# Layernorm in pieces between evictions, one range wrap per table pair, and half-wise hazards in the C scaling of an S5 and Mish kernel

## The chip, the cores and the metric

The kernel runs on one core of one Trainium2 chip. The metric is the device time of one execution in microseconds, and lower is better. Kernels that were sent together ran on the same chip and share their runs of the kernel before.

## The reference, cut to what matters

```python
xn = layernorm(x)                                   # x: 1 x 2048 x 1024, bf16
dt, Lam = exp(log_dt), Lambda_re + 1j * Lambda_im   # 1024 states
Lam_bar = exp(dt * Lam)
Bu = xn @ (((Lam_bar - 1) / Lam)[:, None] * B).T    # B, C complex
h[t] = Lam_bar * h[t-1] + Bu[t]                     # scan over 2048 steps
y = 2 * (h @ C.T).real + xn * Dskip
u = xn @ w1 + b1                                    # 1024 -> 3584 (the B_ half, on the same xn)
out = x + y + (u * tanh(softplus(u))) @ w2
```

## The kernel before

The sequence is handled in four blocks of 512 steps. A block has four stages on TensorE: 28 tiles of first matmuls (8 matmuls each, 224 in all), the projection by B (8 state tiles of 16 matmuls), the second matmuls (224) and the output projection by C (128). VectorE adds the bias to each tile of the first stage while it moves it out of PSUM (`hb`); this move is called the tile's eviction below. ScalarE makes Mish in four groups of seven tiles: Exp, Ln(1 + .), Tanh. The complex recurrence is turned into a real scan by rotating with tables of cosine and sine (`tab`).

The first block has extra work, which a function `side(f)` inserts after tile `f`: the skip product, the next block's layernorm, coefficients, tables, and the transposes of B and C. This is the part that the change rewrites:

```python
def side(f):
    if blk == 0:
        if f == 0:
            for q in range(NQ): ln_skip(0, q)
        if f == 1:
            ln_stats(1, 0); ln_stats(1, 1); ln_apply(1, 0)      # ... the other quarters likewise
            coefficients()
        if f == GF - 1:                      # GF = 7: after Mish group 0 was queued
            for j in range(5): table(j)
            for j in range(5, NJ): phases(j)
        if f == 3 * GF - 1:                  # after Mish group 2
            for j in range(5, NJ): table(j)
        # ... transposes of B (f < 16) and C (f >= 16) on the sync queue

def first_tile(f):
    # 8 matmuls into PSUM bank f % 8 ...
    if f % GF == 0 and f >= 2 * GF:
        mish_mul(f // GF - 2)                # VectorE; waits for ScalarE's Mish of that group
    vop(lambda e: e.tensor_scalar(hb[:, hs, :], ps[:, bank, :], b1(f), None, op0=ALU.add), ...)
    if f % GF == GF - 1:
        mish(f // GF)                        # ScalarE
```

The tables need an angle wrapped into half a turn to either side, which GpSimd does in three operations, for sine and cosine separately:

```python
def phases(j):
    for s in range(2):
        turn = 0.25 if s == 0 else 0.0
        pop(... px = iot * thp[j] + turn)                     # tensor_scalar, mult and add
        pop(... py = (px + ROUND_MAGIC) - ROUND_MAGIC)
        pop(... dst = px - py)
```

The C scaling makes, per state tile and half, two copies on ScalarE and two products on VectorE. Its three buffers rotate, and its hazards (which operation must wait for which, because they touch the same data) are tracked for the whole state tile `b_CT[j]`:

```python
def scale_C(j):
    for h in range(2):
        ta, b_ta = ct[n_ct[0] % 3]; tb, b_tb = ct[(n_ct[0] + 1) % 3]; n_ct[0] += 2
        aop(ta = cim * nci2[j], reads=[b_CT[j], ...], writes=[b_ta])
        aop(tb = cre * nci2[j], reads=[b_CT[j], ...], writes=[b_tb])
        vop(cre = cre * cr2[j] + ta, reads=[b_CT[j], b_ta], writes=[b_CT[j]])
        vop(cim = cim * ncr2[j] + tb, reads=[b_CT[j], b_tb], writes=[b_CT[j]])
```

## Time and profile before

The time before is 678.91 us, the median of three runs (678.77 to 678.99). The span of the profiled run is 676.4 us.

| engine | busy, us | share of the span |
|---|---|---|
| TensorE (PE) | 621.5 | 92% |
| VectorE (DVE) | 478.6 | 71% |
| ScalarE (ACT) | 247.7 | 37% |
| GpSimd (POOL) | 74.9 | 11% |

TensorE is the bound, and what can be gained lies in the time in which it waits. The page's chain that ended last, as shares of the span by engine, says how much of the end was set by others:

```profile
PE 73%; DVE 17%; ACT 7%; issue 1%; DMA 1%; POOL 0%; DVEq 0%; ACTq 0%; POOLq 0%
```

A quarter of the chain is on VectorE and ScalarE. Apart from the last 1.2 us of the run, all of that is in the first block and its start, as the prediction shows with TensorE's waits and timeline.

### The profile page before, as it was taken

To read this page: it belongs to the slowest core of one execution; us is meant where nothing else is said; L and a number is where in the kernel's file an instruction comes from. 1 tells how busy PE (TensorE), PEld (TensorE's weight loads), DVE (VectorE), ACT (ScalarE), POOL (GpSimd) and SP (SyncE) were. 2 spreads that over 40 slices of the span, in tenths; PEclk is the share of its full clock that TensorE was granted. 3 is DMA by queue.
4 is the path that set the end of the run, shared out by engine and by line. 5 is a ranking of instruction groups with operands and counts; after the bars stand their busy time and mean duration, and the time that the engine had idled before them with its cause. 6 is when DMAs were issued, how large, how long until landed. Compare 5 with 4: busy or idle time off the path is not lost.

```text
span 676.4 us, 7254 instructions
## 1 busy us (share of the span) xinstructions
PE 621.5 (92%) x2849; PEld 280.4 (41%) x2849; DVE 478.6 (71%) x718; ACT 247.7 (37%) x163; POOL 74.9 (11%) x74
## 2 busy tenths in 40 slices
PE   0583979999968999999999999999999999999997
PEld 0231434444423444444444444444444444444443
DVE  4698519988887455999983455999983455999702
ACT  2103999722220499500000499500000499400000
POOL 7995360000001000000000000000000000000000
PEclk9995999999997999999999999999999999999999
DMA  9594996077302653019623654018521543014001
GB/s 286 102 211 101 214 245 133 0 194 191 114 0 83 189 155 134 1 60 213 163 63 96 179 156 128 1 65 215 157 63 63 156 155 125 1 65 153 1 0 63
DMA packets 124018, 79.40 MB, mean 117 GB/s; under 512 B 48898, under 2 KB 106256, under 8 KB 123984
## 3 DMA queue, kind: packets, MB, share of 16 engines
q1 hardware_dynamic: 120224, 70.79, 39.5%
q10 hardware_dynamic: 2592, 4.72, 1.9%
q0 software_dynamic: 1168, 3.42, 1.6%
q8 instruction: 23, 0.38, 0.2%
q14 instruction: 11, 0.09, 0.0%
HBM read 63.19 MB, written 4.19 MB: 100 GB/s over the span
## 4 chain that ended last, share of the span: by engine, by line
PE 73%; DVE 17%; ACT 7%; issue 1%; DMA 1%; POOL 0%; DVEq 0%; ACTq 0%; POOLq 0%
PE ps L602 35%; PE ps L526 22%; PE ps L546 16%; DVE hT L566 3%; DVE CT L487 2%; DVE CT L484 2%; DVE stats L337 2%; DVE mt L571 2%; ACT tab L428 1%; DVE xn L354 1%; ACT act L508 1%; ACT act L506 1%; ACT act L507 1%; ACT ct L480 1%; DMA st<-in_B_b_dram 1%
## 5 line engine op out<-in xcount | busy, mean ns | idle before, releaser
L526 PE MATMUL ps<-xnT,ring 128*128 128x512 bf16 x896 | 199.2, 386 | 15.4 <-issue 14.4
L602 PE MATMUL ps<-ring,act 128*128 128x512 bf16 x896 | 194.0, 379 | 0.0
L526 PEld LDWEIGHTS ps<-xnT,ring 128*128 128x128 bf16 x896 | 88.7, 99 | 125.1 <-issue 22.4
L533 DVE TENSOR_SCALAR hb<-ps,par 128x512 bf16<-128x512 f32 x112 | 81.8, 749 | 75.5 <-PE ps L526 74.7
L602 PEld LDWEIGHTS ps<-ring,act 128*128 128x128 bf16 x896 | 87.7, 98 | 105.7
L602 PE MATMUL ps<-CT,hT 128*128 128x512 bf16 x512 | 113.7, 384 | 9.1 <-DVE CT L487 9.1
L546 PE MATMUL ps<-xnT,BT 128*128 128x512 bf16 x512 | 112.7, 382 | 4.4 <-DVE hb L533 4.4
L551 DVE TENSOR_TENSOR mt<-ps,tab 128x1024 bf16<-128x1024 f32 x64 | 75.3, 1219 | 11.4 <-PE ps L546 9.9
L602 PEld LDWEIGHTS ps<-CT,hT 128*128 128x128 bf16 x512 | 50.5, 99 | 71.7 <-DVE CT L487 10.1
L546 PEld LDWEIGHTS ps<-xnT,BT 128*128 128x128 bf16 x512 | 50.4, 99 | 66.0 <-DVE hb L533 4.9
L506 ACT ACTIVATE act<-hb 128x3584 bf16<-128x3584 bf16 x16 | 50.9, 3180 | 50.1 <-DVE hb L533 50.1
L635 DVE TENSOR_TENSOR xx<-ps,xx 128x1024 bf16<-128x1024 f32 x16 | 19.5, 1224 | 56.8 <-PE ps L602 56.7
L566 DVE TENSOR_TENSOR_SCAN hT<-cs,qi,hT 128x512 bf16<-128x512 f32 x48 | 58.9, 1269 | 0.0
L506 ACT ACT_TABLE_LOAD x5 | 6.4, 1283 | 124.4 <-PE ps L526 124.3
L507 ACT ACTIVATE act<-act 128x3584 bf16<-128x3584 bf16 x16 | 51.0, 3190 | 0.2
L508 ACT ACTIVATE act<-act 128x3584 bf16<-128x3584 bf16 x16 | 51.0, 3190 | 0.2
L513 DVE TENSOR_TENSOR act<-act,hb 128x3584 bf16<-128x3584 bf16 x16 | 32.4, 2023 | 20.0 <-ACT act L508 20.0
L571 DVE TENSOR_TENSOR mt<-hT,tab 128x1024 bf16<-128x1024 bf16 x64 | 41.4, 689 | 1.1
L286 POOL DMA_DIRECT2D xx<-in_A_x_dram x12 | 6.6, 553 | 273.0 <-DVE xx L635 265.4
L342 ACT ACTIVATE rs<-rs 128x1 f32<-128x1 f32 x16 | 3.2, 203 | 91.7 <-DVE rs L340 91.7
L420 POOL TENSOR_SCALAR py<-px 128x512 f32<-128x512 f32 x16 | 31.1, 1944 | 1.4
L480 ACT ACTIVATE ct<-CT,cs 128x512 f32<-128x512 bf16 x16 | 11.4, 714 | 51.0 <-DVE CT L487 51.0
(63 smaller groups left out, 306.0 us busy)
## 6 DMA issues: line engine op xcount, KB each, us to landing
ring<-in_B_w_dram SPq DMA_DIRECT2D x112, 512.0 KB, 3.8
out_dram<-xx ACTq DMA_DIRECT2D x16, 256.0 KB, 2.0
xx<-in_A_x_dram POOLq DMA_DIRECT2D x12, 256.0 KB, 4.1
xx<-in_A_x_dram SPq DMA_DIRECT2D x2, 256.0 KB, 3.8
xx<-in_A_x_dram ACTq DMA_DIRECT2D x2, 256.0 KB, 4.1
dsk<-in_A_Dskip_dram POOLq DMA_DIRECT2D x1, 256.0 KB, 6.7
xnT<-xn SPq DMA_TRANSPOSE x12, 4.6
BT<-in_A_B_re_dram SPq DMA_TRANSPOSE x8, 4.9
```

The source lines that it names most:

```text
L420: pop(lambda e: e.tensor_scalar(py[:], px[:], ROUND_MAGIC, ROUND_MAGIC, op0=ALU.add, op1=ALU.subtract), reads=[b_px], writes=[b_py])
L506: aop(lambda e: e.activation(a, hs, AF.Exp), reads=[b_hb[g % 2]], writes=[b_act[g]])
L507: aop(lambda e: e.activation(a, a, AF.Ln, bias=1.0), reads=[b_act[g]], writes=[b_act[g]])
L508: aop(lambda e: e.activation(a, a, AF.Tanh), reads=[b_act[g]], writes=[b_act[g]])
L513: vop(lambda e: e.tensor_tensor(a, a, hs, op=ALU.mult), reads=[b_act[g], b_hb[g % 2]], writes=[b_act[g]])
L526: PE.mm(lambda e, k=k: e.matmul(ps[:, bank, :], lhsT=wt[:, k, fi * P:(fi + 1) * P], rhs=xnT[:, k, :], start=k == 0, stop=k == NK - 1), rea ...
L533: vop(lambda e: e.tensor_scalar(hb[:, hs, :], ps[:, bank, :], b1(f), None, op0=ALU.add), reads=[b_ps[bank], b_par], writes=[b_hbf[hs]])
L546: PE.mm(lambda e, j=j, ci=ci, k=k, bank=bank: e.matmul(ps[:, bank + ci, :], lhsT=BT[:, ci, j, k, :], rhs=xnT[:, k, :], start=k == 0, stop= ...
L551: vop(lambda e, s=s, u=u, j=j: e.tensor_tensor(mt[:, s, :, :], u, tab[:, s, j, :].unsqueeze(1).to_broadcast([P, 2, TB]), op=ALU.mult), rea ...
L566: vop(lambda e, ci=ci, init=init: e.tensor_tensor_scan(out=hT[:, ci, j, :], data0=cj("r", j).to_broadcast([P, TB]), data1=hT[:, ci, j, :], ...
L571: vop(lambda e, s=s: e.tensor_tensor(mt[:, s, :, :], hT[:, :, j, :], tab[:, s, j, :].unsqueeze(1).to_broadcast([P, 2, TB]), op=ALU.mult), ...
L602: PE.mm(lambda e: e.matmul(ps[:, u, :], lhsT=lhsT, rhs=rhs, start=st_, stop=last), reads=reads, writes=[b_ps[u]], first=st_, last=last)
```

## The change

The intent is to keep TensorE fed in block 0. The layernorm of block 1 and the coefficients go in small pieces between evictions; the square root of the layernorms of blocks 1 to 3 leaves ScalarE; one wrap serves both tables of a pair, with the cosine as sin(pi/2 - 2 pi |x|), which costs an Abs on ScalarE; three table pairs come before Mish 0; and the C scaling gets hazards per half and seven buffers.

```diff
-    b_CT = [Buf("CT%d" % j) for j in range(NJ)]
+    b_CT = [Buf("CT%d" % j, parts=[Buf("CT%d_%d" % (j, h)) for h in range(2)]) for j in range(NJ)]
 ...
+    def ln_stats_only(blk, q): ...      # bn_stats twice, bn_aggr
+    def ln_rsqrt(): ...                 # 1/sqrt of all four quarters by shift and three Newton steps, VectorE
+    def ln_scale(blk, q): ...           # (x - mean) * rsqrt
 ...
     def phases(j):
-        for s in range(2):
-            turn = 0.25 if s == 0 else 0.0
-            pop(... tensor_scalar(px, iot, thp[j], turn, op0=mult, op1=add))
-            pop(... tensor_scalar(py, px, ROUND_MAGIC, ROUND_MAGIC, op0=add, op1=subtract))
-            pop(... dst = px - py)
+        pop(... tensor_scalar(px, iot, thp[j], None, op0=mult))
+        pop(... tensor_scalar(py, px, ROUND_MAGIC, -ROUND_MAGIC, op0=add, op1=add))
+        pop(... xs = px - py)
     def table(j):
-        for s in range(2): aop(tab[s, j] = Sin(2 pi * ph[j, s]))
+        aop(tab[1, j] = Sin(2 pi * src))
+        aop(src = Abs(src))
+        aop(tab[0, j] = Sin(-2 pi * src + pi / 2))
 ...
     def scale_C(j):                      # buffers: 3 -> NCT = GF = 7
-                reads=[b_CT[j], ...], writes=[b_CT[j]]
+                reads=[b_CT[j].parts[h], ...], writes=[b_CT[j].parts[h]]
 ...
         def side(f):
-            # f == 0: four skips; f == 1: whole layernorm of block 1, all coefficients
-            # f == 6: tables 0 to 4; f == 20: tables 5 to 7
+            if f < NQ: ln_skip(0, f)
+            if f == 4: coefficients(0)
+            if f == 5: tables 0 to 2            # queued before Mish 0
+            if f == 7: tables 3 to 7            # queued after Mish 0
+            if 6 <= f < 9: coefficients(f - 5)
+            if f in (9, 10, 11, 12): ln_stats_only(1, f - 9)
+            if f == 13: ln_rsqrt()
+            if f in (16, 17, 18, 19): ln_scale(1, f - 16)
 ...                                       # blocks 1 and 2 use the new layernorm form too
```

More of the change, by code (lines that the diff above doesn't have):

```diff
@@ L11 @@
 TWO_PI = 6.283185
+HALF_PI = 1.5707963
 ROUND_MAGIC = 12582912.0
@@ L268, in build_kernel, with ph_slot @@
     ph = [scratch("ph_%s%d" % w, w[0], w[1], f32, TB)
-          for w in (("h", 2), ("h", 3), ("h", 6), ("h", 7), ("a", 11), ("a", 12), ("a", 13),
-                    ("h", 0), ("h", 1), ("h", 4), ("h", 5))]
-    def ph_slot(j, s):
-        return ph[(2 * j + s) % len(ph)]
+          for w in (("h", 0), ("h", 1), ("h", 2), ("h", 3), ("h", 6), ("h", 7), ("a", 11), ("a", 12))]
+    def ph_slot(j):
+        return ph[j]
     vop, aop, pop = VE.op, AC.op, PO.op
@@ L325, in build_kernel @@
                                   compare_op=ALU.is_equal, fill=0.0), reads=[b_ident], writes=[b_ident])
-    pop(lambda e: e.memset(kon[:, 1:2], 0.0), writes=[b_kon])
+    pop(lambda e: e.memset(kon[:, 0:1], HALF_PI), writes=[b_kon])
+    pop(lambda e: e.memset(kon[:, 1:2], 0.0), reads=[b_kon], writes=[b_kon])
     pop(lambda e: e.iota(iot_i[:], pattern=[[1, TB]], base=0, channel_multiplier=0), writes=[b_iot_i])
@@ L356, in ln_apply, with ln_stats_only, ln_rsqrt, ln_scale @@
             reads=[b_xx[i][q], b_mv[q], b_rs[q]], writes=[b_xn[q]])
+    rv = [sb("rv%d" % i, [P, NQ], f32 if i < 3 else i32) for i in range(4)]
+    b_rv = [Buf("rv%d" % i) for i in range(4)]
+    def ln_stats_only(blk, q):
+        i, s = blk % 2, q % 2
+        for h in range(2):
+            vop(lambda e, h=h: e.bn_stats(stats[:, s, h, :], xx[:, i, q, h * 512:(h + 1) * 512]),
+                reads=[b_xx[i][q]], writes=[b_stats[s]])
+        vop(lambda e: e.bn_aggr(mv[:, q, :], stats[:, s, :, :]), reads=[b_stats[s]], writes=[b_mv[q]])
+    def ln_rsqrt():
+        v, y, t = (rv[n][:, :] for n in range(3))
+        yi, vi, b_i = rv[1][:, :].bitcast(i32), rv[0][:, :].bitcast(i32), rv[3][:, :]
+        vop(lambda e: e.tensor_scalar(v, mv[:, :, 1], EPS, None, op0=ALU.add), reads=b_mv, writes=[b_rv[0]])
+        vop(lambda e: e.tensor_scalar(b_i, vi, 1, None, op0=ALU.logical_shift_right),
+            reads=[b_rv[0]], writes=[b_rv[3]])
+        vop(lambda e: e.tensor_scalar(yi, b_i, -1.0, float(0x5f3759df), op0=ALU.mult, op1=ALU.add),
+            reads=[b_rv[3]], writes=[b_rv[1]])
+        for _ in range(3):
+            vop(lambda e: e.tensor_tensor(t, y, y, op=ALU.mult), reads=[b_rv[1]], writes=[b_rv[2]])
+            vop(lambda e: e.tensor_tensor(t, t, v, op=ALU.mult), reads=[b_rv[0], b_rv[2]], writes=[b_rv[2]])
+            vop(lambda e: e.tensor_scalar(t, t, -0.5, 1.5, op0=ALU.mult, op1=ALU.add),
+                reads=[b_rv[2]], writes=[b_rv[2]])
+            vop(lambda e: e.tensor_tensor(y, y, t, op=ALU.mult), reads=[b_rv[1], b_rv[2]], writes=[b_rv[1]])
+    def ln_scale(blk, q):
+        i = blk % 2
+        vop(lambda e: e.tensor_scalar(xn[:, q, :], xx[:, i, q, :], mv[:, q, 0:1], rv[1][:, q:q + 1],
+                                      op0=ALU.subtract, op1=ALU.mult),
+            reads=[b_xx[i][q], b_mv[q], b_rv[1]], writes=[b_xn[q]])
     def ln_skip(blk, q):
@@ L414, in phases @@
     def phases(j):
-        for s in range(2):
-            dst, b_dst = ph_slot(j, s)
-            turn = 0.25 if s == 0 else 0.0
-            pop(lambda e, turn=turn: e.tensor_scalar(px[:], iot[:], cj("thp", j), turn, op0=ALU.mult, op1=ALU.add),
-                reads=[b_iot, b_cs["thp"]], writes=[b_px])
-            pop(lambda e: e.tensor_scalar(py[:], px[:], ROUND_MAGIC, ROUND_MAGIC, op0=ALU.add, op1=ALU.subtract),
-                reads=[b_px], writes=[b_py])
-            pop(lambda e, dst=dst: e.tensor_tensor(dst[:], px[:], py[:], op=ALU.subtract),
-                reads=[b_px, b_py], writes=[b_dst])
@@ L425, in table @@
-    def table(j):
-        for s in range(2):
-            src, b_src = ph_slot(j, s)
-            aop(lambda e, s=s, src=src: e.activation(tab[:, s, j, :], src[:], AF.Sin, scale=TWO_PI, bias=kon[:, 1:2]),
-                reads=[b_src, b_kon], writes=[b_tab[j]])
-    def coefficients():
-        smalls("ys", "thp", ROUND_MAGIC, ROUND_MAGIC, ALU.add, ALU.subtract)
+        xs, b_xs = ph_slot(j)
+        pop(lambda e: e.tensor_scalar(px[:], iot[:], cj("thp", j), None, op0=ALU.mult),
+            reads=[b_iot, b_cs["thp"]], writes=[b_px])
@@ new lines, in phases @@
+        pop(lambda e: e.tensor_scalar(py[:], px[:], ROUND_MAGIC, -ROUND_MAGIC, op0=ALU.add, op1=ALU.add),
+            reads=[b_px], writes=[b_py])
+        pop(lambda e: e.tensor_tensor(xs[:], px[:], py[:], op=ALU.subtract),
+            reads=[b_px, b_py], writes=[b_xs])
+    def table(j):
+        src, b_src = ph_slot(j)
+        aop(lambda e: e.activation(tab[:, 1, j, :], src[:], AF.Sin, scale=TWO_PI, bias=kon[:, 1:2]),
+            reads=[b_src, b_kon], writes=[b_tab[j]])
+        aop(lambda e: e.activation(src[:], src[:], AF.Abs), reads=[b_src], writes=[b_src])
+        aop(lambda e: e.activation(tab[:, 0, j, :], src[:], AF.Sin, scale=-TWO_PI, bias=kon[:, 0:1]),
+            reads=[b_src, b_kon], writes=[b_tab[j]])
@@ L433, in coefficients, with turns @@
+    def turns():
+        smalls("ys", "thp", ROUND_MAGIC, -ROUND_MAGIC, ALU.add, ALU.add)
         small("xs", "thp", "ys", ALU.subtract)
-        smalls("xc", "thp", 0.25, None, ALU.add, ALU.bypass)
-        smalls("yc", "xc", ROUND_MAGIC, ROUND_MAGIC, ALU.add, ALU.subtract)
-        small("xc", "xc", "yc", ALU.subtract)
+        smalls("xc", "xs", -1.0, None, ALU.mult, ALU.bypass)
+        small("xc", "xs", "xc", ALU.max)
         aop(lambda e: e.activation(c("s1"), c("xs"), AF.Sin, scale=TWO_PI, bias=kon[:, 1:2]),
@@ L438, in coefficients @@
             reads=[b_cs["xs"], b_kon], writes=[b_cs["s1"]])
-        aop(lambda e: e.activation(c("c1"), c("xc"), AF.Sin, scale=TWO_PI, bias=kon[:, 1:2]),
+        aop(lambda e: e.activation(c("c1"), c("xc"), AF.Sin, scale=-TWO_PI, bias=kon[:, 0:1]),
             reads=[b_cs["xc"], b_kon], writes=[b_cs["c1"]])
-        small("lr", "r", "c1", ALU.mult)
-        small("li", "r", "s1", ALU.mult)
-        smalls("nr", "lr", -1.0, None, ALU.add, ALU.bypass)
-        small("den", lre, lre, ALU.mult)
@@ L446, in coefficients @@
-        small("t1", lim, lim, ALU.mult)
-        small("den", "den", "t1", ALU.add)
-        vop(lambda e: e.reciprocal(c("inv"), c("den")), reads=[b_cs["den"]], writes=[b_cs["inv"]])
-        small("t1", "nr", lre, ALU.mult)
-        small("t2", "li", lim, ALU.mult)
-        small("t1", "t1", "t2", ALU.add)
-        small("t1", "t1", "inv", ALU.mult)
-        smalls("cr2", "t1", 2.0, None, ALU.mult, ALU.bypass)
-        smalls("ncr2", "t1", -2.0, None, ALU.mult, ALU.bypass)
-        small("t1", "li", lre, ALU.mult)
@@ L456, in coefficients @@
-        small("t2", "nr", lim, ALU.mult)
-        small("t1", "t1", "t2", ALU.subtract)
-        small("t1", "t1", "inv", ALU.mult)
-        smalls("nci2", "t1", -2.0, None, ALU.mult, ALU.bypass)
+    def coefficients(part):
+        if part == 0:
+            small("den", lre, lre, ALU.mult)
+            small("t1", lim, lim, ALU.mult)
+            small("den", "den", "t1", ALU.add)
+            vop(lambda e: e.reciprocal(c("inv"), c("den")), reads=[b_cs["den"]], writes=[b_cs["inv"]])
+        if part == 1:
+            small("lr", "r", "c1", ALU.mult)
+            small("li", "r", "s1", ALU.mult)
+            smalls("nr", "lr", -1.0, None, ALU.add, ALU.bypass)
+        if part == 2:
+            small("t1", "nr", lre, ALU.mult)
+            small("t2", "li", lim, ALU.mult)
+            small("t1", "t1", "t2", ALU.add)
+            small("t1", "t1", "inv", ALU.mult)
+            smalls("cr2", "t1", 2.0, None, ALU.mult, ALU.bypass)
+            smalls("ncr2", "t1", -2.0, None, ALU.mult, ALU.bypass)
+        if part == 3:
+            small("t1", "li", lre, ALU.mult)
+            small("t2", "nr", lim, ALU.mult)
+            small("t1", "t1", "t2", ALU.subtract)
+            small("t1", "t1", "inv", ALU.mult)
+            smalls("nci2", "t1", -2.0, None, ALU.mult, ALU.bypass)
@@ L461, in build_kernel @@
+    turns()
     for j in range(NJ):
-        if j == 5:
-            break
         phases(j)
     base_hb = nc.lookup_mloc(hb).addr
-    ct = []
-    for i in range(3):
-        ct.append((nc.alloc_sbuf_tensor_at("ct%d" % i, [P, HB], f32, offset=base_hb + 2048 * i),
-                   Buf("ct%d" % i, parts=b_hbf[2 * i:2 * i + 2])))
+    NCT = GF
+    ct = [(nc.alloc_sbuf_tensor_at("ct%d" % i, [P, HB], f32, offset=base_hb + 2048 * i),
+           Buf("ct%d" % i, parts=b_hbf[2 * i:2 * i + 2])) for i in range(NCT)]
@@ L476, in scale_C @@
             cre, cim = (CT[:, ci, j, h * HB:(h + 1) * HB] for ci in range(2))
-            ta, b_ta = ct[n_ct[0] % 3]
-            tb, b_tb = ct[(n_ct[0] + 1) % 3]
+            b_c = b_CT[j].parts[h]
+            ta, b_ta = ct[n_ct[0] % NCT]
+            tb, b_tb = ct[(n_ct[0] + 1) % NCT]
             n_ct[0] += 2
             aop(lambda e, ta=ta, cim=cim: e.activation(ta[:], cim, AF.Copy, scale=cj("nci2", j)),
-                reads=[b_CT[j], b_cs["nci2"]], writes=[b_ta])
+                reads=[b_c, b_cs["nci2"]], writes=[b_ta])
             aop(lambda e, tb=tb, cre=cre: e.activation(tb[:], cre, AF.Copy, scale=cj("nci2", j)),
-                reads=[b_CT[j], b_cs["nci2"]], writes=[b_tb])
+                reads=[b_c, b_cs["nci2"]], writes=[b_tb])
             vop(lambda e, ta=ta, cre=cre: e.scalar_tensor_tensor(
                 out=cre, in0=cre, scalar=cj("cr2", j), in1=ta[:], op0=ALU.mult, op1=ALU.add),
-                reads=[b_CT[j], b_ta, b_cs["cr2"]], writes=[b_CT[j]])
+                reads=[b_c, b_ta, b_cs["cr2"]], writes=[b_c])
             vop(lambda e, tb=tb, cim=cim: e.scalar_tensor_tensor(
                 out=cim, in0=cim, scalar=cj("ncr2", j), in1=tb[:], op0=ALU.mult, op1=ALU.add),
-                reads=[b_CT[j], b_tb, b_cs["ncr2"]], writes=[b_CT[j]])
+                reads=[b_c, b_tb, b_cs["ncr2"]], writes=[b_c])
     def transpose_B(j):
@@ L647, in side @@
         def side(f):
-            if blk == 0:
-                if f == 0:
-                    for q in range(NQ):
-                        ln_skip(0, q)
-                if f == 1:
-                    ln_stats(1, 0)
-                    ln_stats(1, 1)
-                    ln_apply(1, 0)
-                    ln_stats(1, 2)
-                    ln_apply(1, 1)
-                    ln_stats(1, 3)
-                    ln_apply(1, 2)
-                    ln_apply(1, 3)
-                    coefficients()
-                if f == GF - 1:
-                    for j in range(5):
-                        table(j)
-                    for j in range(5, NJ):
-                        phases(j)
-                if f == 3 * GF - 1:
-                    for j in range(5, NJ):
-                        table(j)
-                if f < 16 and f % 2 == 0:
-                    transpose_B(f // 2)
-                if f >= 16:
-                    transpose_C(f - 16)
+            if blk:
+                return
+            if f < NQ:
+                ln_skip(0, f)
+            if f == 4:
+                coefficients(0)
+            if f == 5:
+                for j in range(3):
+                    table(j)
+            if f == 7:
+                for j in range(3, NJ):
+                    table(j)
+            if 6 <= f < 9:
+                coefficients(f - 5)
+            if f in (9, 10, 11, 12):
+                ln_stats_only(1, f - 9)
+            if f == 13:
+                ln_rsqrt()
+            if f in (16, 17, 18, 19):
+                ln_scale(1, f - 16)
+            if f < 16 and f % 2 == 0:
+                transpose_B(f // 2)
+            if f >= 16:
+                transpose_C(f - 16)
         for f in range(NF):
@@ L683, in build_kernel @@
             for q in range(NQ):
-                ln_stats(blk + 1, q)
-                if q:
-                    ln_apply(blk + 1, q - 1)
-            ln_apply(blk + 1, NQ - 1)
+                ln_stats_only(blk + 1, q)
+            ln_rsqrt()
+            for q in range(NQ):
+                ln_scale(blk + 1, q)
         for j in range(NJ):
```

## The prediction

> **What bounds the kernel now.** I read the busy slices first, then TensorE's waits and timeline, then the clock in chosen windows, then VectorE's and ScalarE's timelines around each hole. TensorE is busy 92% of the span, and its timeline shows the last three blocks (216.5 us to the end) as one unbroken stream: 48.35 us of first matmuls, 27.6 of projection, 48.35 of second matmuls, 27.6 of output projection, 152 us a block, with no wait. So blocks 1 to 3 can't get shorter by anything in this diff. The waits of TensorE (waiter, releaser: total us, times, longest) all lie in block 0 and its start:
>
> ```profile
> PE ps L526 <- issue: 14.4, 1, 14.4
> PE ps L404 <- DVE xn L354: 13.6, 4, 7.1
> PE ps L602 <- DVE CT L487: 9.1, 2, 7.8
> PE ps L546 <- DVE hb L533: 4.4, 1, 4.4
> ```
>
> Its timeline (start, length, work, idle before it) places the holes:
>
> ```profile
> 27.47 19.99 PE L526 MATMUL ps<-xnT,ring 128*128 128x512 bf16 x80 [0.99 <-DVE xnT L411]
> 61.84 33.69 PE L526 MATMUL ps<-xnT,ring 128*128 128x512 bf16 x144 [14.38 <-issue]
> 95.36 1.89 PE L546 MATMUL ps<-xnT,BT 128*128 128x512 bf16 x8
> 101.64 27.41 PE L546 MATMUL ps<-xnT,BT 128*128 128x512 bf16 x120 [4.38 <-DVE hb L533]
> ...
> 205.69 11.01 PE L602 MATMUL ps<-CT,hT 128*128 128x512 bf16 x40 [7.80 <-DVE CT L487]
> ```
>
> The 14.4 us hole follows the tenth tile. "issue" hides its cause: eight PSUM banks plus the two evicted ones are used up, and VectorE does all of the next layernorm and the coefficients from 39.63 to 61.08 before it evicts tile 2, at 60.99, just before TensorE goes on.
>
> The 4.4 us hole: tile 21's eviction stands behind the Mish product of group 1, which waits for ScalarE. ScalarE's timeline between the two Mish groups is full:
>
> ```profile
> 64.41 3.19 ACT L506 ACTIVATE act<-hb 128x3584 bf16<-128x3584 bf16 x1 [4.68 <-DVE hb L533]
> ...
> 76.62 1.28 ACT L428 ACT_TABLE_LOAD   x1
> 77.91 2.96 ACT L428 ACTIVATE tab<-ph_h,kon 128x512 bf16<-128x512 f32 x4
> ...
> 86.47 3.19 ACT L506 ACTIVATE act<-hb 128x3584 bf16<-128x3584 bf16 x1
> ```
>
> The 9.1 us hole (1.3 and 7.8) is the scaling of C. VectorE spends 8.83 us per state tile in recurrence and scaling, of which 1.47 is a wait for ScalarE, eight times:
>
> ```profile
> 140.03 0.75 DVE L487 SCALAR_TENSOR_TENSOR CT<-CT,cs,ct 128x512 bf16<-128x512 bf16 x1
> 142.26 0.75 DVE L484 SCALAR_TENSOR_TENSOR CT<-CT,cs,ct 128x512 bf16<-128x512 bf16 x1 [1.47 <-ACT ct L482]
> 143.05 0.75 DVE L487 SCALAR_TENSOR_TENSOR CT<-CT,cs,ct 128x512 bf16<-128x512 bf16 x1
> 143.72 2.33 DVE L566 TENSOR_TENSOR_SCAN hT<-cs,hT 128x512 bf16<-128x512 f32 x2
> ```
>
> Each hole also costs clock afterwards. The windows (stretch, length, busy us and count per engine, granted clock) right after the two long holes:
>
> ```profile
> 61.80:66.00 4.20, 4.16 (x10) 1.49 (x11) 4.20 (x7) 1.59 (x1) 0.00 (x0) 0.50 0.00 0
> 205.70:210.00 4.30, 4.30 (x11) 1.54 (x12) 4.09 (x12) 0.00 (x0) 0.00 (x0) 0.50 0.01 4
> ```
>
> **What the Trainium skill says.** (1) TensorE: Matmul & The Clock Gate, section "What's actually happening": after an idle window of about 3.4 us the array runs at half clock until about 3.4 us of activity. The trace agrees: clock 0.50 and 10 or 11 matmuls in 4.2 us, where the steady rate is 48.35/224 = 0.216 us each. So 144 matmuls took 33.5 us from start to the next group's start against 31.1, and the last 40 took 10.84 against 8.63: 2.4 and 2.2 us lost. (2) ScalarE: Activation LUTs, section "Table sets: the hidden batching unit": the tables are loaded by set, and cheap functions, copy and abs among them, are in every set. Copy agrees: the scaling copies start at 129.75 straight after Tanh, without a load. Abs doesn't occur before the change, so no run shows it yet. A load takes 1.28 us here. (3) SBUF — State Buffer, section "Who interferes with whom": a VectorE instruction with two SBUF inputs contends with GpSimd reads. The trace agrees: the four skip additions L364 took 0.69, 1.64, 0.98 and 0.69 us while GpSimd was at its range wraps.
>
> **The change part by part.**
>
> *Layernorm and coefficients in pieces.* VectorE's new side work is 4 skips (one after each of tiles 0 to 3), 4 small operations after tile 4, 14 in three portions after tiles 6 to 8, statistics of one quarter (two of 0.7 us and one of 0.2, so 1.7 with gaps) after each of tiles 9 to 12, 15 chained small operations of about 0.19 after tile 13, and four normalizations of 0.6 to 0.9 after tiles 16 to 19. With 14 evictions of 0.67 (9.4), the skips as measured with GpSimd beside them (31.83 to 39.05: 7.2), 18 small at 0.18 (3.2), 4 x 1.7 (6.8) and 2.8, VectorE needs 29.4 us up to tile 13, from 31.1 to 60.5. A tile takes TensorE 8 x 0.216 = 1.73 us, so it finishes tile 13 at 27.47 + 2.56 + 14 x 1.73 = 54.2 (2.56 is the cold start: 80 matmuls lasted 19.83 in place of 17.27). VectorE is 6 us behind at worst, 3.6 tiles, against eight banks. So the 14.4 us hole and the 2.4 us of cold clock go away whole: 16.8.
>
> *Tables.* Removed on GpSimd: one wrap of three operations per table pair (48 operations become 24), off the path. Added on ScalarE: one Abs per pair. Three pairs move before Mish 0, into free time: ScalarE is free from 26.2, runs the two small sines, then 3 x 2.15 = 6.5 us, and is done near 36. Five pairs remain between Mish 0 and Mish 1. In the old trace 10 sines took 7.26 us (a dependent one 0.73, an independent one 0.61). In the new code all three operations of a pair depend on each other, Abs being in place, so a pair takes 0.61 + 2 x 0.73 + gaps = 2.15, and five take 10.8. That is 3.5 us more than before.
> Mish 0 starts with the eviction of tile 6: 31.1 + 7 x 0.67 + 7.2 + 0.7 = 43.7. From there: 12.2 (three activations of 3.19 and two loads, to the end), 1.3 load, 10.8 tables, 1.3 load, 12.2 Mish 1: 37.8, so 81.5. Product and eviction of tile 21 took 2.94 before TensorE restarted (98.70 to 101.64), so bank 5 is free at 84.5. TensorE, no longer held up, finishes tile 27 at 27.47 + 2.56 + 28 x 1.73 = 78.4 and the first half of state tile 0 at 80.1. The **new hole is 84.5 - 80.1 = 4.4 us**, as long as the old one: TensorE and ScalarE both move forward. This part gives nothing by itself, but the projection starts at 84.5 in place of 101.64, 17.1 earlier, its own warm-up unchanged.
>
> *C scaling.* Hazards per half and seven buffers in place of three let ScalarE run ahead, so the 1.47 us go: 8.83 becomes 2.37 + 1.33 + 0.67 (recurrence) + 4 x 0.74 = 7.35 per state tile. VectorE enters the recurrence at 134.88 - 17.1 = 117.8 and ends state tile 7 at 117.8 + 8 x 7.35 = 176.6. TensorE's second matmuls end at 177.22 - 17.1 = 160.1, and it first needs state tile 7 after 80 + 8 more matmuls, at 160.1 + 88 x 0.216 = 179.1. So 2.5 us are in hand and the 9.1 us hole closes, with its 2.2 us of cold clock: 11.3.
>
> *Layernorm of blocks 1 and 2.* 36 VectorE instructions in 12.2 us (298.26 to 310.48) become 31 in 4 x 1.7 + 2.8 + 4 x 0.5 = 11.6, and ScalarE loses its Sqrt and its loads. TensorE waits for none of it: 0.
>
> **Sum.** 160.1 + 128 x 0.216 = 187.7 for the end of block 0, where block 1 began at 216.53: 28.8 us. By terms: 14.4 + 2.4 + 0 + 9.1 + 2.2 = 28.1. I take 28.6: 678.9 - 28.6 = 650.3.
>
> **Rivals.**
> 1. *Abs reloads tables.* If Sin and Abs were not in one set here, each of the five pairs would cost two loads more: 12.8 us. Mish 1 would end at 94.3 and the hole be 17 us: near 663. The skill speaks against it; only copy is shown. Chance 4%.
> 2. *Scaling stays in step.* If VectorE kept 8.83 per state tile (say, by buffers that come free late), it would end at 117.8 + 70.6 = 188.4, 9.3 us after TensorE wants it, with a cold restart: near 661. Against it: four ScalarE copies cost 2.7 us per state tile, far under 7.35, and ScalarE has been idle since Mish 3.
> 3. *Transfers become the bound.* From 33.74 to 56 the sync queue issued one weight load and two transposes per 4.4 us; TensorE without holes uses one weight load per 3.45 us. If the ring had no lead, block 0 would lose 13 x 0.95 = 12 us: 662. For it: DMA is at 1.1 of its mark there and SP issues back to back. Against it: seven items are loaded ahead; the eighth is issued at 33.7 and wanted at 54, the fourteenth is issued near 60 and wanted at 75, and the C transposes end near 100, before the 117 at which they are scaled. Hidden, by my count.
> 4. *ScalarE gets through sooner.* If the skips meet fewer GpSimd reads, Mish 0 starts near 42.7, and the hole falls under 3.4 us and may keep its clock warm: 648.
>
> **Range and chances.** The two large terms rest on measured holes with margins of several microseconds; the open term is the hole before the projection, 3 to 6 us with or without a cold restart (2 us). That gives 647 to 654. Rivals 1 to 3 together have some 8% and end between 661 and 664, still over 2% faster (that line is 665.3). Faster 0.95, same 0.04, slower 0.01.
>
> **What would show it.** Right: TensorE's waits list one hole of 3 to 6 us at the projection, released by the eviction of tile 21, and no 14 us one; Sin, Abs and Sin of a pair at 0.6 to 0.73 each without a load between; VectorE at some 7.35 us per state tile without a ScalarE wait; blocks 1 to 3 unchanged at 152 us. Wrong: a weight-ring or transpose wait in block 0, loads before Abs, a wait for the C scaling in the output projection, or a hole between tiles 8 and 20.

## The result, and the profile after

The changed kernel took 649.22 us (median of 4 runs, 648.98 to 650.07), beside 678.95 us for the kernel before (four runs, one more than above). The ratio is 0.9563, with a 95% interval of 0.9547 to 0.958. The predicted value was 650.3.

The chain that ended last, of the changed kernel, is now almost all TensorE:

```profile
PE 92%; DVE 4%; ACT 2%; DMA 1%; issue 0%; POOL 0%; DVEq 0%; POOLq 0%
```

Within block 0's four stages TensorE has one wait left that is longer than 1 us (waiter, releaser: total us, times, longest). L585 is the projection and L565 the first matmuls, which were L546 and L526:

```profile
PE ps L585 <- DVE hb L572: 5.9, 1, 5.9
```

Its timeline in block 0 (start, length, work, idle before it):

```profile
25.44 50.51 PE L565 MATMUL ps<-xnT,ring 128*128 128x512 bf16 x224 [0.99 <-DVE xnT L444]
75.79 1.89 PE L585 MATMUL ps<-xnT,BT 128*128 128x512 bf16 x8
83.61 28.01 PE L585 MATMUL ps<-xnT,BT 128*128 128x512 bf16 x120 [5.93 <-DVE hb L572]
111.45 48.51 PE L641 MATMUL ps<-ring,act 128*128 128x512 bf16 x224
159.80 27.79 PE L641 MATMUL ps<-CT,hT 128*128 128x512 bf16 x128
```

The hole after the tenth tile is gone, and so is the one in the output projection. The hole before the projection is still there, and it is longer: 5.93 us in place of 4.38. Stage by stage, from the starts in the two timelines:

| stage of block 0 | before, us | after, us | gain, us |
|---|---|---|---|
| up to the first matmul | 27.47 | 25.44 | 2.03 |
| first matmuls, 224 | 67.89 | 50.35 | 17.54 |
| projection by B | 33.52 | 35.66 | -2.14 |
| second matmuls | 48.34 | 48.35 | -0.01 |
| output projection by C | 39.31 | 27.63 | 11.68 |
| block 0 | 216.53 | 187.43 | 29.10 |

Blocks 1 to 3 and the end took 676.4 - 216.53 = 459.9 us before and 647.2 - 187.43 = 459.8 after. The whole gain is in block 0.

ScalarE's timeline of the changed kernel between Mish 0 and Mish 1 shows the new pair (Sin, Abs, Sin), with one table load ahead of the five pairs:

```profile
55.58 1.28 ACT L460 ACT_TABLE_LOAD   x1
56.88 0.72 ACT L460 ACTIVATE tab<-ph_h,kon 128x512 bf16<-128x512 f32 x1
57.63 0.63 ACT L462 ACTIVATE ph_h<-ph_h 128x512 f32<-128x512 f32 x1
58.30 0.72 ACT L463 ACTIVATE tab<-ph_h,kon 128x512 bf16<-128x512 f32 x1
...
67.15 1.28 ACT L545 ACT_TABLE_LOAD   x1
68.44 3.19 ACT L545 ACTIVATE act<-hb 128x3584 bf16<-128x3584 bf16 x1
```

No load stands between Sin and Abs. The pairs fill 56.88 to 67.13: five in 10.25 us. The activation that starts at 68.44 is the first of Mish 1, and ScalarE did not stop for a moment between Mish 0 and Mish 1.

The chain in order of time reads differently at this point. It puts the wait for Mish 1 down to an eviction (start, us, what):

```profile
67.79 0.67 DVE hb L572
68.46 3.17 ACT act L545
```

That is a coincidence of times. This eviction, of tile 20, ends at 68.45, a hundredth of a microsecond after the activation had begun; Mish 1 reads tiles 7 to 13, the last of which was moved out by 57.01. What the activation came after was ScalarE's own table load, which ends at 68.43. The experiments with the tables settle this.

VectorE's timeline in the C scaling of the changed kernel has no wait left:

```profile
122.36 0.75 DVE L526 SCALAR_TENSOR_TENSOR CT<-CT,cs,ct 128x512 bf16<-128x512 bf16 x1
123.03 0.75 DVE L523 SCALAR_TENSOR_TENSOR CT<-CT,cs,ct 128x512 bf16<-128x512 bf16 x1
123.81 0.75 DVE L526 SCALAR_TENSOR_TENSOR CT<-CT,cs,ct 128x512 bf16<-128x512 bf16 x1
124.48 2.33 DVE L605 TENSOR_TENSOR_SCAN hT<-cs,hT 128x512 bf16<-128x512 f32 x2
```

From this scan to the next one, at 131.76, are 7.28 us, in place of 8.83.

One thing had not been foreseen: the first matmul starts 2.03 us sooner. The chain in order of time shows where. These are the normalizations of the first three quarters of block 0's own layernorm, before:

```profile
14.86 0.94 DVE xn L354
...
19.00 0.94 DVE xn L354
...
23.14 0.94 DVE xn L354
```

and after:

```profile
15.11 0.55 DVE xn L355
...
18.17 0.55 DVE xn L355
...
21.35 0.55 DVE xn L355
```

A quarter took 4.14 us before and takes 3.06 to 3.18 now, though its VectorE code is the same. Only what GpSimd does beside it was changed. Two small operations of VectorE in the trace of before, and the GpSimd operations of the same moments, show what they waited for:

```profile
13.38 0.66 DVE L349 SCALAR_TENSOR_TENSOR rs<-rs 128x1 f32<-128x1 f32 x1
...
14.26 0.56 DVE L353 TENSOR_TENSOR rs<-rs 128x1 f32<-128x1 f32 x1
```

```profile
12.76 1.26 POOL L422 TENSOR_TENSOR ph_h<-px,py 128x512 f32<-128x512 f32 x1
14.13 0.69 POOL L418 TENSOR_SCALAR px<-iot,cs 128x512 f32<-128x512 f32 x1
```

The first ends at 14.04 and the second at 14.82, when the GpSimd operation beside it ends (14.02 and 14.82). With no GpSimd work, in the layernorms that run during blocks 1 and 2, the same operations take 0.22 and 0.16 us, the normalization 0.55 in place of 0.94, and a whole quarter 3.05 (302.62 to 305.67).

### The profile page after: what moved, and what is told of

Read it like the earlier page. It is cut to its first block, busy times and chain, and to the rows that moved or that the text cites. A ratio compares the mean times of both kernels' runs of the same rounds, so it can differ in the third digit from the quotient of the medians.

```text
span 647.2 us, 7184 instructions
## 1 busy us (share of the span) xinstructions
PE 616.4 (95%) x2849; PEld 279.6 (43%) x2849; DVE 470.2 (73%) x702; ACT 243.3 (38%) x153; POOL 50.7 (8%) x51
## 4 chain that ended last, share of the span: by engine, by line
PE 92%; DVE 4%; ACT 2%; DMA 1%; issue 0%; POOL 0%; DVEq 0%; POOLq 0%
PE ps L641 47%; PE ps L565 28%; PE ps L585 17%; DMA st<-in_B_b_dram 1%; DVE hb L572 1%; DVE stats L338 1%; ACT act L547 0%; ACT act L546 0%; ACT act L545 0%; DVE xn L355 0%; DVE act L552 0%; DVE xn L387 0%; DVE rs L354 0%; POOL st L295 0%; ACT L547 0%
## 5 line engine op out<-in xcount | busy, mean ns | idle before, releaser
L565 PE MATMUL ps<-xnT,ring 128*128 128x512 bf16 x896 | 196.0, 382 | 1.0 <-DVE xnT L444 1.0
L565 PEld LDWEIGHTS ps<-xnT,ring 128*128 128x128 bf16 x896 | 88.1, 98 | 108.2 <-issue 3.6
L585 PE MATMUL ps<-xnT,BT 128*128 128x512 bf16 x512 | 113.3, 384 | 5.9 <-DVE hb L572 5.9
L641 PE MATMUL ps<-CT,hT 128*128 128x512 bf16 x512 | 111.2, 379 | 0.0
L585 PEld LDWEIGHTS ps<-xnT,BT 128*128 128x128 bf16 x512 | 50.5, 99 | 68.0 <-DVE hb L572 6.4
L546 ACT ACTIVATE act<-act 128x3584 bf16<-128x3584 bf16 x16 | 51.0, 3191 | 0.2
L605 DVE TENSOR_TENSOR_SCAN hT<-cs,hT 128x512 bf16<-128x512 f32 x16 | 18.7, 1208 | 0.0
```

What stands on the lines that cost most here:

```text
L546: aop(lambda e: e.activation(a, a, AF.Ln, bias=1.0), reads=[b_act[g]], writes=[b_act[g]])
L565: PE.mm(lambda e, k=k: e.matmul(ps[:, bank, :], lhsT=wt[:, k, fi * P:(fi + 1) * P], rhs=xnT[:, k, :], start=k == 0, stop=k == NK - 1), rea ...
L585: PE.mm(lambda e, j=j, ci=ci, k=k, bank=bank: e.matmul(ps[:, bank + ci, :], lhsT=BT[:, ci, j, k, :], rhs=xnT[:, k, :], start=k == 0, stop= ...
L605: vop(lambda e, ci=ci, init=init: e.tensor_tensor_scan(out=hT[:, ci, j, :], data0=cj("r", j).to_broadcast([P, TB]), data1=hT[:, ci, j, :], ...
L641: PE.mm(lambda e: e.matmul(ps[:, u, :], lhsT=lhsT, rhs=rhs, start=st_, stop=last), reads=reads, writes=[b_ps[u]], first=st_, last=last)
```

## The experiments

All eleven runs gave correct results. The theory is this: the time is TensorE's work plus its holes in block 0. The first hole comes from the order of VectorE's work, the last from the hazards of the C scaling, and the middle one from ScalarE's chain between Mish 0 and Mish 1, which also swallows the earlier start. The rivals are named with each run. Where two kernels of different calls are compared, I use the difference of their ratios times 679 us.

### lump: VectorE's work in one piece again

```diff
-            if f < NQ: ln_skip(0, f)
+            if f == 0: all four ln_skip(0, q)
+            if f == 1:
+                four ln_stats_only(1, q); ln_rsqrt(); four ln_scale(1, q); coefficients(0 to 3)
-            (the same calls after tiles 4, 6 to 13 and 16 to 19)
```

> The changed kernel with its layernorm of block 1 and all coefficients in one piece again after tile 1 (skips in one piece after tile 0), everything else as changed. If the order of VectorE's work is what closed the 14.4 us hole: tile 2 is evicted near 54 us, TensorE waits about 10 us at the eleventh tile and restarts cold, Mish 0 moves to about 57 us and the projection restarts near 97.5 in place of 83.6: about 663 us. Rival, that the smaller amount of VectorE work closed it: no hole, 649 us.

Measured: 664.72 us, ratio 0.9788 (0.9773 to 0.9802). TensorE's waits in its trace:

```profile
PE ps L565 <- issue: 11.3, 1, 11.3
...
PE ps L585 <- DVE hb L572: 7.6, 1, 7.6
```

The hole at the eleventh tile is back with the same amount of work, so it is the order that makes it; the amount sets its length (11.3 us here, 14.4 with the longer piece of the kernel before). The expectation was 10 us for the hole and 663 us for the time. The hole before the projection is 1.6 us longer than in the profile of the changed kernel. The cost against the changed kernel is (0.9788 - 0.9563) x 679 = 15.3 us.

### scale_whole and scale_3buf: hazards or buffers

```diff
# scale_whole
-            b_c = b_CT[j].parts[h]
+            b_c = b_CT[j]
# scale_3buf
-    NCT = GF
+    NCT = 3
```

> The changed kernel, C scaling with seven buffers but hazards on the whole state tile again. If the hazards were what held VectorE in step with ScalarE: a ScalarE wait of 1.47 us in each state tile comes back, 8.83 us a tile, the recurrence ends near 188 where TensorE wants it at 179: hole of 9 us and cold restart of 2 us, about 660.5 us. Rival, that three buffers were the limit: no wait, 649 us.

> The changed kernel, C scaling with hazards per half but three buffers. If the hazards alone do it: ScalarE's second copy of a half waits for a buffer but is still ready 0.7 us before VectorE wants it, 7.3 us a tile, no hole, 649 us. Rival, that buffers are needed: VectorE waits again, up to 8.8 us a tile, up to 660 us.

Measured: scale_whole 661.08 us, ratio 0.9727 (0.9709 to 0.9746), and scale_3buf 649.54 us, ratio 0.9566 (0.9552 to 0.9581). VectorE's timeline of scale_whole has the old wait in each state tile:

```profile
122.60 0.75 DVE L523 SCALAR_TENSOR_TENSOR CT<-CT,cs,ct 128x512 bf16<-128x512 bf16 x1 [1.47 <-ACT ct L521]
```

In its trace TensorE waits 8.9 us in the output projection. In that of scale_3buf it does not wait there, and a state tile takes 7.37 us (scans at 118.62 and 125.99). The hazards per half are worth (0.9727 - 0.9563) x 679 = 11.1 us; the four additional buffers are worth nothing that these runs can show.

### scale_alone: one part on the kernel before

```diff
# on the kernel before
+    the changed b_CT with halves, NCT = GF, scale_C as changed
```

> The kernel before with only the C scaling changed (hazards per half, seven buffers). The sum of the prediction gives this part 9.1 us of hole and 2.2 of cold clock: 678.9 - 11.3 = 667.6 us, with the 14.4 and 4.4 us holes unchanged. Rival, that the parts only pay together: near 679.

Measured: 667.82 us, ratio 0.9836 (0.982 to 0.9853), so 11.1 us off. TensorE's output projection runs without a wait, and the two other holes stay (14.0 and 4.0 us). Alone or with the rest, this part is worth the same. The 15.3 us of lump and these 11.1 make 26.4 of the 29.7 us by which the medians differ. What is left, 3.3 us, is what lump still has ahead of the kernel before, beyond the C scaling. The profiles account for 2.3 of it (second matmuls from 126.59 in place of 128.88): the first matmul starts 2.1 us sooner and the first hole is 3.1 us shorter, since the piece of VectorE work that makes it is shorter, but the hole before the projection is 3.2 us longer.

### tab4, tab5, tab5_late: where the table pairs stand

```diff
# tab4: 4 pairs before Mish 0, 4 between;  tab5: 5 before, 3 between
             if f == 5:
-                for j in range(3): table(j)
+                for j in range(4): table(j)          # tab5: 5
             if f == 7:
-                for j in range(3, NJ): table(j)
+                for j in range(4, NJ): table(j)      # tab5: 5
# tab5_late: 5 before, the other 3 after Mish 2
-            if f == 7:
+            if f == 3 * GF - 1:
                 for j in range(5, NJ): table(j)
```

> The changed kernel with four table pairs before Mish 0 and four between Mish 0 and Mish 1 (three and five as changed). If ScalarE's chain from Mish 0 to Mish 1 sets the projection's start, one pair less (2.05 us) shrinks the hole from 5.9 to 3.9 us, perhaps still followed by a half clock: 647.2 us. Rival, that the hole comes from VectorE or a transfer: 649.2.

> The changed kernel with five table pairs before Mish 0 and three between. By the ScalarE theory the hole shrinks to 1.8 us, short enough to keep the clock up: 4.1 us of hole plus up to 1.9 us of cold clock, 643.2 us; if the clock cost stays, 645.1. Rival: 649.2.

> The changed kernel with five table pairs before Mish 0, none between Mish 0 and Mish 1, and three after Mish 2. By the ScalarE theory tile 21 is evicted near 72 us, before TensorE wants its bank at 77.5; the hole is gone, block 0 runs without a wait and ends near 179.4 in place of 187.4: 641.2 us. Rival, that with the hole gone another thing holds TensorE (C transposes, weight ring, Mish product of group 3, tables 5 to 7 late): between 642 and 649, with a new wait in TensorE's list.

| kernel | pairs between Mish 0 and Mish 1 | hole, us | time, us | ratio (95%) |
|---|---|---|---|---|
| changed | 5 | 5.93 | 649.22 | 0.9563 (0.9547 to 0.958) |
| tab4 | 4 | 3.80 | 647.40 | 0.9532 (0.9516 to 0.9547) |
| tab5 | 3 | 1.91 | 644.29 | 0.9483 (0.9469 to 0.9497) |
| tab5_late | 0 | none | 641.66 | 0.944 (0.9426 to 0.9454) |

One pair moved takes 2.1 us off the hole in these profiles, the next 1.9, as the ScalarE theory says. One profile fixes the hole only to about a microsecond, though: up to the projection the changed kernel, scale_whole, scale_3buf and ln_old (below) are the same, and their profiles show 5.93, 4.62, 4.98 and 6.40 us. So the times and tab5_late carry the argument more than the single steps: the intervals of the changed kernel and tab4 just touch, those of tab4, tab5 and tab5_late are apart, and with no pairs in ScalarE's chain the hole is gone. In tab5_late Mish 1 starts at 57.91, after the eviction of its last tile, with the first matmul at 26.30; so the eviction of tile 20 was never what it needed. The timeline of TensorE in tab5_late has no hole at all in block 0:

```profile
26.30 50.76 PE L565 MATMUL ps<-xnT,ring 128*128 128x512 bf16 x224 [0.99 <-DVE xnT L444]
76.89 27.79 PE L585 MATMUL ps<-xnT,BT 128*128 128x512 bf16 x128
104.52 48.51 PE L641 MATMUL ps<-ring,act 128*128 128x512 bf16 x224
152.87 27.79 PE L641 MATMUL ps<-CT,hT 128*128 128x512 bf16 x128
```

The step from tab4 to tab5 also saves clock. The windows right after the hole's end (stretch, length, busy us and count per engine in the order of the page, granted clock, DMA share, GB/s), of tab4 and then of tab5:

```profile
82.00:84.00 2.00, 2.00 (x6) 0.73 (x5) 2.00 (x4) 1.99 (x2) 0.00 (x0) 0.50 1.25 107
```

```profile
80.00:82.00 2.00, 2.00 (x10) 0.92 (x11) 2.00 (x4) 1.97 (x3) 0.00 (x0) 1.00 1.05 247
```

After 3.80 us of idle TensorE ran at half clock, after 1.91 it did not. What a restart costs can be read off the runs as the time from the restart to the second matmuls, less 120 x 0.216 = 25.9 us:

| kernel | hole before the projection, us | restart to second matmuls, us | lost, us |
|---|---|---|---|
| tab5 | 1.91 | 25.91 | 0.0 |
| tab4 | 3.80 | 27.27 | 1.4 |
| scale_alone | 4.02 | 27.60 | 1.7 |
| wrap_add (next section) | 4.23 | 28.74 | 2.8 |
| before | 4.38 | 27.24 | 1.3 |
| scale_whole | 4.62 | 28.15 | 2.2 |
| scale_3buf | 4.98 | 28.80 | 2.9 |
| changed | 5.93 | 27.84 | 1.9 |
| ln_old | 6.40 | 27.38 | 1.5 |
| lump | 7.57 | 27.26 | 1.4 |

The loss is there or not there; it doesn't grow with the hole. In tab5 a new wait of 0.8 us shows 26 matmuls into the second matmuls, for VectorE's last rotation, which the expected 643.2 us had not counted; tab5_late does without it: its tile 21 is moved out sooner, and VectorE starts the projection's products at 80.55 in place of 83.74.

The two-sided placement of tab5_late, five pairs early and three late, is 1.3% faster than the changed kernel (ratios 0.944 and 0.9563) and faster than tab5 (0.9483). It was repeated: 641.36 us, ratio 0.9444 (0.9431 to 0.9456).

> The same kernel as tab5_late, beside the next one on the same chip, to compare a third of a per cent: 641.5 us, no hole in block 0.

### wrap_add and tab5_late_wrap: why the start came sooner, and what it is worth

```diff
 def phases(j):
-        pop(... tensor_scalar(px, iot, thp[j], None, op0=mult))
+        pop(... tensor_scalar(px, iot, thp[j], 0.0, op0=mult, op1=add))
```

> The changed kernel with the first operation of GpSimd's wrap as multiply and add 0 in place of multiply alone. In the trace of before that form took 0.69 us and a wrap 4.15 us, the same as one quarter of the first layernorm on VectorE; the changed one takes 1.57 to 1.89 and 5.2 us, and the first layernorm ends 2.0 us sooner. If the two engines' equal period is the cause, the wrap goes back to 4.15 us, the layernorm to 4.15 us a quarter, and the first matmul to about 27.4 us; the end moves by under 1 us, since the hole before the projection shrinks by the same: 649.2 to 650.2. Rival, that the start counts in full: 651.2; rival, that the start has another cause: first matmul stays at 25.4.

> tab5_late with GpSimd's wrap in the 4.15 us form of wrap_add. In wrap_add the first matmul came 2.1 to 2.2 us later and the end moved by 1 us at most, which I put down to the hole before the projection taking it up. If that is right, here, with no hole, the later start counts in full: first matmul near 27.8 to 28.5, time 2.1 us over tab5_late_again. Rival, that the start is taken up by something else: within 0.5 us of it.

In wrap_add the `px` operation takes 0.69 us (median of its eight) in place of 1.66, a wrap 4.15 in place of about 5.2, and a quarter of the layernorm is back at 4.14:

```profile
15.06 0.94 DVE L355 TENSOR_SCALAR xn<-xx,mv,rs 128x1024 bf16<-128x1024 bf16 x1
...
19.20 0.94 DVE L355 TENSOR_SCALAR xn<-xx,mv,rs 128x1024 bf16<-128x1024 bf16 x1
```

The first matmul starts at 27.67. This one operand form, and nothing that the change meant to do, brought the 2 us. The faster form on GpSimd is the slower one for the kernel. A quarter of the layernorm takes VectorE 3.05 us when GpSimd is idle; with the faster form it took 4.14 us, which is the period of a wrap (4.15): three operations of each quarter (two small ones and the normalization) meet a GpSimd operation, and VectorE is held to GpSimd's step. With the slower form, whose wraps come every 5.1 to 5.5 us, the quarters take 3.06 to 3.18 and meetings are few. The operand form as the cause is shown by the run; the meetings are read from the times at which operations end.

What it is worth depends on the hole. In wrap_add the hole before the projection shrinks to 4.23 us, and the time is 650.26 us, ratio 0.9567 (0.9553 to 0.9581), against 0.9563 for the changed kernel: nothing that the intervals can tell. In tab5_late_wrap, with no hole, the first matmul starts at 28.23 against 26.03, and the time is 643.89 us, ratio 0.9475 (0.9462 to 0.9488), against 0.9444 for tab5_late on the same chip (tab5_late_again): 0.0031 x 679 = 2.1 us, all of it. Both came as expected.

### ln_old: the layernorm form in blocks 1 and 2

```diff
         if 0 < blk < NB - 1:
-            four ln_stats_only(blk + 1, q); ln_rsqrt(); four ln_scale(blk + 1, q)
+            the old ln_stats and ln_apply, with the square root on ScalarE
```

> The changed kernel with the old layernorm form (square root on ScalarE, quarter by quarter) in blocks 1 and 2. It costs VectorE about 0.9 us more a block between the projection and the recurrence, and ScalarE table loads, but TensorE waits for neither: 649.2 us, blocks 1 and 2 at 151.9 us. Rival, that part of the gain came from there: 650 to 651.

Measured: 649.57 us, ratio 0.956 (0.9547 to 0.9573), against 0.9563. Blocks 1 to 3 take the same time (block 1's four stages, from 187.00 to 338.94, are 151.9 us). In blocks 1 and 2 the new form does nothing for the time.

## Why the prediction was right or wrong, point by point

**The bound and the size: right.** 649.22 us were measured and 650.3 predicted, with TensorE's unbroken stream from the projection's restart on and blocks 1 to 3 unchanged.

**The layernorm in pieces: right.** No hole stands in the first 224 matmuls. VectorE was through with tile 13's side work at 59.9 in place of the 60.5 worked out. Together with the first start's shorter warm-up (2.0 us over the steady 48.36, in place of 2.56) and the restart that is no longer needed, the stage gained 17.5 us where 16.8 were predicted; the run lump shows the cause.

**The tables: the mechanism right, the size of the hole off.** The 4.4 us hole came out as 5.93. The failing step is "TensorE, no longer held up, finishes tile 27 at 27.47 + 2.56 + 28 x 1.73 = 78.4": it took the start of before for granted, and tile 27 was done at 75.8, of which 2.0 us are the earlier start and the rest the shorter warm-up. ScalarE came sooner too, but by less. Mish 0 started at 43.37 in place of 43.7, and five pairs took 10.25 us in place of 10.8, because an Abs takes 0.63 us and I had given it the 0.73 of a dependent sine. So the projection restarted at 83.61 in place of 84.5. For the Abs the Trainium skill would have given the right size: ScalarE: Activation LUTs, section "What ACT_TABLE_LOAD costs", says that each pointer operand of an activation adds some 93 ns, and the Abs has no pointer for its bias where the sine has one; the trace shows 0.63 against 0.72. The miss of 1.5 us is that of one profile; the four profiles with the same code up to there show holes of 4.62 to 6.40 us, all above the 4.4. No run went back to two wraps per pair, so what the shared wrap itself is worth was not tested: five pairs took ScalarE 7.26 us before and 10.25 after, and as an estimate from these two numbers the Abs makes its chain 3.0 us longer.

**The C scaling: right.** 7.28 us per state tile in place of 7.35, and state tile 7 was ready 3.3 us ahead (VectorE ends its scaling at 175.5; TensorE wants it at 159.8 + 88 x 0.216 = 178.8), where 2.5 were predicted. The gain of 11.3 was measured as 11.1 us alone and 11.1 us by undoing. That the diff has two causes for it, hazards and buffers, was not taken apart in the prediction; the hazards are all of it.

**The layernorm of blocks 1 and 2: right.** Nothing, shown by ln_old.

**The rivals.** Abs does not reload tables. Scaling does not stay in step. Transfers did not become the bound: the sync queue still issues a weight load and two transposes in some 4.4 us, the fifteenth item goes out at 62.1, and the last transpose of C is issued at 93.7, ahead of VectorE's first scaling at 121.6. The fourth, an earlier Mish 0, came half true, 0.3 us, but TensorE came sooner by more. How early Mish 0 comes varies from run to run: in the profile of scale_whole the eight skip operations took 7.25 us in place of 8.51, and Mish 0 began at 41.08 in place of 43.37.

**What the prediction did not see.** GpSimd's wrap was put "off the path". Its count of operations is; its timing was not, since the first layernorm, on the path to the first matmul, contends with it. The prediction quoted exactly this contention, but only for the skips. The 2 us were then lost again in the hole before the projection, so that the total came out right by two misses that offset each other: 2.03 us sooner at the start, and 2.14 us longer in the projection. The cancelling has a cause, since the hole takes up the start (wrap_add and tab5_late_wrap), but the prediction foresaw neither, so in that much the closeness of the total is luck.

## What to carry to other kernels

When two engines race towards the same point, a gain on one of them is only a longer wait, so work out both arrival times and look at what the later one has in front of it; here TensorE's earlier start was lost in the hole, and moving table work out of ScalarE's chain gave another 1.3%. Track hazards at the grain at which the work is done, before adding buffers. And where VectorE and GpSimd work side by side in loops, VectorE can be held to GpSimd's step; here one operand form on GpSimd, 5.2 us a wrap in place of 4.15, was worth 2 us on the path.

## What the Trainium skill lacked or had wrong

- GPSIMD Engine Reference: I found no figure on it for `tensor_scalar`. On 128 x 512 f32 with a pointer scalar, multiply and add took 0.69 us in most of its calls, and multiply alone 1.57 to 1.89, as told above. Why the form with one operation is the slower one stays open.
- SBUF — State Buffer, section "Who interferes with whom": its rule that two-input VectorE operations contend with GpSimd reads agrees with the traces, but it gives no size for small ones. Operations on 128 x 1 that take 0.16 to 0.22 us alone mostly took 0.52 to 0.66 beside GpSimd, and up to 1.27, ending together with the GpSimd operation beside them; with the slowed normalizations that was 2 us of layernorm on the path.
- ScalarE: Activation LUTs, section "What ACT_TABLE_LOAD costs": it counts 2.66 us for a switch of sets, of which 1.38 are a drain. In these traces a switch costs 1.31 us from the end of one activation to the start of the next: Mish 1's Exp ends at 71.63 and its Ln starts at 72.94. The load alone is 1.28, as the section says.
- TensorE: Matmul & The Clock Gate, section "What's actually happening": the idle limit of about 3.4 us agrees (1.91 us of idle kept the clock, 3.80 did not). It gives some 3.4 us as the time that a restart runs at half clock, which by an estimate from this figure would lose 1.7 us; it does say that the window runs freely and that the number of slow matmuls varies from run to run. Here the loss was 1.3 to 2.9 us, not growing with the hole; in wrap_add all of 84 to 90 us ran at a granted clock of 0.50 and the restart was at 84.24, so the cold stretch can last 5.8 us.
